# Four layers of linear attention and MLP on one core: turned blocks by way of DRAM, earlier queries, key maxima from PSUM, and row statistics on ScalarE

## The chip, the cores and the metric

One core of one Trainium2 chip runs the kernel. The metric is device time in microseconds (us). The engines go by the names of the profile: PE is TensorE, DVE VectorE, ACT ScalarE, POOL GpSimd, SP SyncE, which issues the DMA transfers. "PEld" is TensorE's weight load.

## The reference

2048 rows of 576 numbers pass through four layers, in turn a linear attention (A) and an MLP (B), with the same weights both times. Each layer adds its result to its input. Cut to what is computed:

```python
phi = lambda t: jnp.where(t > 0, t + 1, jnp.exp(t)) + 1e-6
def A(x, wqkv, wo):                 # 32 heads of 18
    q, k, v = split(x @ wqkv)
    pq, pk = phi(q), phi(k)
    kv  = einsum("bhsd,bhse->bhde", pk, v)
    z   = einsum("bhsd->bhd", pk)
    num = einsum("bhqd,bhde->bhqe", pq, kv)
    den = einsum("bhqd,bhd->bhq", pq, z) + 1e-6
    return (num / den) @ wo
def B(x, w1, b1, w2, b2):           # 576 -> 4608 -> 576
    return gelu(x @ w1 + b1) @ w2 + b2
x = x + A(layernorm(x)); x = x + B(layernorm(x))
x = x + A(layernorm(x)); x = x + B(layernorm(x))
```

The result is in bfloat16.

## The kernel before

Layers are counted 1 to 4 here; in the code `li` runs from 0 to 3, so layers 1 and 3 are attention (`layer_A`) and layers 2 and 4 MLP (`LayerB`). The 2048 rows are 16 tiles of 128 rows, or 4 blocks of 512. The weights stay in SBUF. `yT` holds the normalised rows of the current layer with the features on the partitions, as 5 groups of 128 (the fifth is half full; for the MLP its second half repeats the first). The rows themselves (float32) lie in DRAM as `x_d` between layers; `x_ring` has 5 buffers for rows that come back to be added, `xn` 3 buffers for new sums (`residual`, L372 to L386; the last layer's are called `xbf`).

**Attention.** The key loop goes over 16 tiles: keys (`k_proj`, L400, two halves of 288 columns), values (`v_proj`, L412 and L415), the product of keys and values of the tile before (L430), and from the fifth tile on one query product (`q_proj`, L436), in both layers. There are 20 query products, for 5 groups of heads by 4 blocks. Each half of the keys and each query product goes through phi (L350 to L354): ACT reads PSUM twice, for the exponential and for the number plus 1; DVE takes a minimum and the maximum of the two. Then come sums by head, the products `kvwo` (L481), and for each block the denominators (`den_stage`, L496, with the 1e-6 added by a product of one row at L500, reciprocals by DVE at L504) and five products `rden_ps` (`scale_stage`, L512) that spread the reciprocals over the rows of a group; ACT copies them and DVE multiplies the queries. The output loop has 16 tiles of ten products `wo_ps` (L523), with the reciprocal products of the next block, queries that are left, and the denominators of the block after next between them (at the third tile of a block).

**MLP.** Each of 4 blocks first makes 36 hidden groups (L624, written to `h_ps` and `hp_ps`, GELU by ACT at L620), then four output tiles of 72 products `m_ps` (L672). Two accumulators, `accA` and `accB`, take turns from tile to tile; so the third tile needs the first one's sum.

**Normalisation.** `LNPipe` takes a tile through steps, one at each `tick`: load, statistics on DVE (L272 to L283), the power -1/2 on POOL (L288), shift on POOL where needed (L292), normalisation (L303 on POOL or L307 on DVE) into one of three `y_ring` buffers, then the turn to `yT`. The first block of an MLP is fed from the output loop of the attention: normalised on POOL, turned by PE (`tp`, L324) and copied by ACT. All other blocks, and the attention's rows after the MLP, are turned by DVE in squares of 32 (L225) into one buffer, `turned`, and then moved by 16 transfers of 32 partitions (L232) inside SBUF. One `turned` buffer serves all of these, so a turn waits for the transfers of the block before.

The order of each engine's work is planned by the framework from the program order and the dependencies; PE's order is fixed as written. Some loads and statistics carry an extra order (`after`) behind the last residual sum: before, only those for the second block of an MLP. PSUM has three buffers "h" for keys, queries, denominators, reciprocals and hidden groups, one for `tp`, and the two accumulators.

Of the kernel before, what the change touches and what calls it, by code (L numbers as in the profile page):

```python
# [15 lines left out]
P = 128  # L16
# [18 lines left out]
def build(tc, A_x, A_wqkv, A_wo, B_w1, B_b1, B_w2, B_b2, out, dbg=None, n_layers=4):  # L35
    nc = tc.nc
    dbg = dbg or {}
    with ExitStack() as ctx:
        const = ctx.enter_context(tc.tile_pool(name="const", bufs=1))
        ps_h = ctx.enter_context(tc.tile_pool(name="ps_h", bufs=3, space=PSUM))  # L40
        ps_tp = ctx.enter_context(tc.tile_pool(name="ps_tp", bufs=1, space=PSUM))
# [21 lines left out]
        eps_row = const.tile([1, H], BF16, name="eps_row")  # L63
        one_row = const.tile([1, P], BF16, name="one_row")
# [9 lines left out]
        def inner_diag(tile_, lead, n):  # L74
# [10 lines left out]
            fill(eps_row, 1e-6),  # L85
# [25 lines left out]
        NV = 3  # L111
# [3 lines left out]
        turned = const.tile([P, 4 * KD, TPC, 32], BF16, name="turned")  # L115
        x_d = dpool.tile([NT, P, D], F32, name="x_d")

# [99 lines left out]
        state = dict(ycnt=0, vcnt=0, xl=0)  # L217
        pool_last = dict(norm=None)
        dve_last = dict(norm=None, sum=None, phi=None)

        def turn_rows(y, t, kind):

            c, j = divmod(t, TPC)
            nb = 4 * KD if kind == "B" else D // 32
            nc.vector.transpose(out=turned[:, 0:nb, j, :], in_=y[:, 0:32 * nb])  # L225
            if j < TPC - 1:
                return
            for i in range(4):
                for jj in range(4):
                    nk = KD if 16 + jj < nb else KD - 1  # L230
                    cols = slice(c * CB + i * P, c * CB + (i + 1) * P)
                    nc.sync.dma_start(  # L232
                        out=yT[32 * jj:32 * (jj + 1), 0:nk, cols],
                        in_=turned[32 * i:32 * (i + 1), jj:4 * (nk - 1) + jj + 1:4].rearrange("p k t c -> p k (t c)"))
# [8 lines left out]
        class LNPipe:  # L243
# [3 lines left out]
            def feed(self, xt, t, kind, norm_eng, evac_eng="dve", load_from=None, after=None):  # L247
                self.items.append(dict(stage=(0 if load_from is None else -1), xt=xt, t=t, kind=kind,
                                       norm=norm_eng, evac=evac_eng, load=load_from,
                                       after=after))  # L250

            def busy(self):
                return len(self.items)

            def tick(self, transposes=1):
                for it in list(self.items):
# [5 lines left out]
                    if st == -1:  # L262
# [5 lines left out]
                        it["xt"] = xn  # L268
                    elif st == 0:
# [20 lines left out]
                    elif st == 2 and it["norm"] != "dve":  # L290
                        nmr = work.tile([P, 1], F32, name="ln_nmr", bufs=4)
                        nc.gpsimd.tensor_scalar(out=nmr[:], in0=it["mv"][:, 0:1], scalar1=-1.0,  # L292
                                                scalar2=it["rstd"][:, 0:1], op0=ALU.mult, op1=ALU.mult)
                        it["nmr"] = nmr
                    elif st in (2, 3):
                        y = y_ring[state["ycnt"] % NY]
                        state["ycnt"] += 1
# [12 lines left out]
                        if it["kind"] == "B":  # L310
                            nc.gpsimd.tensor_copy(out=y[:, D:DPAD], in_=y[:, 4 * P:D])
# [3 lines left out]
                    elif st == 4:  # L315
                        y = it["y"]
                        t = it["t"]
                        if it["evac"] == "dma":
                            turn_rows(y, t, it["kind"])
                            self.items.remove(it)  # L320
                            continue
                        tp = ps_tp.tile([P, KD, P], BF16, name="tp", tag="tp")
                        for k in range(KD):
                            pe(nc.tensor.transpose(out=tp[:, k, :], in_=y[:, k * P:(k + 1) * P], identity=ident[:]))  # L324
                        if it["evac"] == "act":
                            nc.scalar.copy(out=yT[:, :, t * P:(t + 1) * P], in_=tp[:])
                        else:
                            nc.vector.tensor_copy(out=yT[:, :, t * P:(t + 1) * P], in_=tp[:])
                        self.items.remove(it)
                        continue  # L330
                    it["stage"] = st + 1

            def drain(self):
                while self.items:
                    self.tick()
# [4 lines left out]
        def warm_table(func, after):  # L340
            warm = nc.scalar.activation(out=act_dummy[:, 0:1], in_=neg_half[:, 0:1], func=func)
            tc.add_manual_dep(warm.ins, after, NOSYNC, reason="table of the next stage loaded early")

# [28 lines left out]
        def residual(li, t, halves):  # L372
            xo = xo_of.pop((li, t))
            last = (li == n_layers - 1)
            if last:
                xn = work.tile([P, 2 * D], BF16, name="xbf", tag="xn", bufs=3)[:, 0:D]
            else:
                xn = work.tile([P, D], F32, name="xn", tag="xn", bufs=3)[:]
            total = nc.vector.tensor_tensor(out=xn.rearrange("p (h n) -> p h n", h=2), in0=halves,  # L379
                                            in1=xo.rearrange("p (h n) -> p h n", h=2), op=ALU.add)  # L380
            dve_last["sum"] = total.ins.name
            if last:
                nc.sync.dma_start(out=out_f[t * P:(t + 1) * P, :], in_=xn)
                return None
            nc.sync.dma_start(out=x_d[t], in_=xn)
            return xn  # L386

        def layer_A(li, next_kind, pre_a1=None):
# [5 lines left out]
            def k_proj(t):  # L394
                tok = slice(t * P, (t + 1) * P)
                pk = blk.tile([P, D], BF16, name="pk", tag="blk")
                for half in range(2):
                    kp = ps_h.tile([P, 512], F32, name="k_ps", tag="h")
                    for k in range(KD):
                        pe(nc.tensor.matmul(kp[:, 0:HALF], lhsT=yT[:, k, tok],  # L400
                                         rhs=wqkv_sb[:, k, D + half * HALF: D + (half + 1) * HALF],
                                         start=(k == 0), stop=(k == KD - 1)))
                    phi_from_psum(kp[:, 0:HALF], pk[:, half * HALF:(half + 1) * HALF], P, HALF)
# [40 lines left out]
            for t in range(NT):  # L444
# [8 lines left out]
                if t >= 4:  # L453
                    q_proj(*q_left.pop(0))
# [62 lines left out]

            def wo_stage(t):
# [8 lines left out]
                if xn is not None and next_kind == "B" and t < TPC:  # L527
                    lnp.feed(xn, t, "B", "pool", "act")
# [20 lines left out]
            for t in range(NT):  # L549
# [9 lines left out]
                if j == 2 and c + 2 < NCA:  # L559
                    den_stage(c + 2)  # L560
                if t == NT - 3:
                    warm_table(ACT.Gelu_apprx_tanh, act_last["copy"])
# [12 lines left out]
        class LayerB:  # L575
# [70 lines left out]
            def run(self):  # L646
                li, next_kind = self.li, self.next_kind

                def feed_next(c, i):
                    if c + 1 < NCB:  # L650
                        t = (c + 1) * TPC + i
                        lnp.feed(None, t, "B", "dve", "dma", load_from=t, after=(dve_last["sum"] if c == 0 else None))

                for c in range(NCB):
# [12 lines left out]
                    for j in range(TPC):  # L667
                        t = c * TPC + j
                        acc = ps_acc.tile([P, 2, 512], F32, name="m2_ps", tag=next_acc())
                        for f in range(NF):  # L670
                            for half in range(2):
                                pe(nc.tensor.matmul(acc[:, half, 0:HALF], lhsT=hT[f][:, j * P:(j + 1) * P],  # L672
                                                    rhs=w2_sb[:, f, half * HALF:(half + 1) * HALF],
                                                    start=(f == 0), stop=(f == NF - 1)))
# [111 lines left out]
```

## Time and profile before

| what | us |
|---|---|
| median of 3 runs (lowest, highest) | 790.73 (789.31, 791.21) |
| the profiled execution, its time | 790.27 |
| the profiled execution, its span | 788.6 |
| PE busy in it | 769.9 |
| layer 1, to the MLP's first product | 0 to 112.10 |
| layer 2, four blocks | 112.10 to 393.84 |
| layer 3 | 393.84 to 491.91 |
| layer 4, first block | 491.91 to 573.47 |
| layer 4, last product of the last tile ends | 784.92 |

In timelines a line gives the start, the length, the engine, the source line, the operation with output and inputs, the count, and in brackets the idle time before it and what ended it. In groups it is the busy total, the mean length of one in ns, and the idle time before with its releasers. Instructions of one kind overlap somewhat, so work is counted here from start to start: 1.23 us for an output tile's ten products, 0.216 for a reciprocal product, 0.56 for a block's denominators, 0.28 for a tile's transposes, 1.08 for a query product. Line numbers in the profile before are those of the kernel before.

### The profile page before, as it was taken

How to read it: one execution, taken by the hardware profiler on the slowest of the kernel's cores; microseconds unless marked ns; L12 is line 12 of the kernel's file. 1: busy time of each engine (PE TensorE's matmuls, PEld its weight loads, DVE VectorE, ACT ScalarE, POOL GpSimd, SP SyncE). 2: the span in 40 equal slices, each digit the busy share in tenths (PEclk: the TensorE clock that was granted, in tenths of full speed). 3: DMA queues.
4: the chain of work that ended last, by engine and by line, in shares of the span. 5: the costliest groups of instructions: out<-in, count | busy, mean ns of one | idle time of the engine just before them, and what ended most of it. 6: DMA issues, size and time to landing. Idle time of an engine off the chain costs nothing.

```text
span 788.6 us, 15939 instructions
## 1 busy us (share of the span) xinstructions
PE 769.9 (98%) x6613; PEld 496.5 (63%) x6613; DVE 275.4 (35%) x710; ACT 341.7 (43%) x754; POOL 127.0 (16%) x211
## 2 busy tenths in 40 slices
PE   8999999999999999999999999996999999999998
PEld 5776654675477457547777756455744764675476
DVE  6786864044324413301355597544100000000000
ACT  5888636304610650362077774650056016304600
POOL 4671403013000301200000022311110010001000
PEclk9999999999999999999999999998899999999999
DMA  9990473122412331311120028443410110011000
GB/s 265 280 294 5 130 252 91 22 75 66 94 43 69 83 65 46 91 17 31 61 61 2 1 89 288 152 94 79 86 39 1 31 61 2 5 50 38 1 24 23
DMA packets 70642, 63.23 MB, mean 80 GB/s; under 512 B 37418, under 2 KB 55210, under 8 KB 70570
## 3 DMA queue, kind: packets, MB, share of 16 engines
q1 hardware_dynamic: 70570, 62.21, 28.1%
q8 instruction: 52, 0.85, 0.4%
q14 instruction: 20, 0.16, 0.1%
HBM read 39.38 MB, written 16.52 MB: 71 GB/s over the span
## 4 chain that ended last, share of the span: by engine, by line
PE 83%; DVE 7%; DMA 4%; SPq 3%; POOL 1%; issue 1%; ACT 1%; DVEq 0%; POOLq 0%
PE m_ps L672 34%; PE h_ps L624 17%; PE hp_ps L624 14%; PE q_ps L436 5%; PE k_ps L400 5%; PE v_ps L415 3%; SPq L232 3%; PE v_ps L412 2%; PE wo_ps L523 2%; DVE xn L379 1%; DMA x_d<-xn 1%; DVE turned L225 1%; PE kvacc L430 1%; DMA x_ring<-x_d 1%; DVE y_ring L307 1%
## 5 line engine op out<-in xcount | busy, mean ns | idle before, releaser
L672 PE MATMUL m_ps<-w_sb,hT 128*128 128x288 bf16 x2304 | 286.2, 287 | 8.5 <-DVE xbf L379 8.5
L672 PEld LDWEIGHTS <-hT 128*128 128x128 bf16 x2304 | 225.9, 98 | 69.8 <-issue 12.1
L624 PEld LDWEIGHTS <-w_sb 64*128 64x128 bf16 x2304 | 124.4, 94 | 136.6 <-issue 1.9
L624 PE MATMUL hp_ps<-yT,w_sb 64*128 64x512 bf16 x1152 | 178.0, 376 | 0.0
L629 ACT COPY relay_sb<-relay_sb 128x1 f32<-128x1 f32 x144 | 28.5, 198 | 276.6 <-PE h_ps L624 234.7
L624 PE MATMUL h_ps<-yT,w_sb 64*128 64x512 bf16 x1152 | 147.9, 376 | 0.0
L620 ACT ACTIVATE hT<-h_ps,b1T 128x512 bf16<-128x512 f32 x144 | 91.2, 684 | 44.5 <-PE h_ps L624 44.5
L288 POOL TENSOR_TENSOR ln_rstd<-ln_u,neg_half 128x1 f32<-128x1 f32 x64 | 36.2, 567 | 413.9 <-DVE ln_u L281 216.8
L620 ACT ACTIVATE hT<-hp_ps,b1T 128x512 bf16<-128x512 f32 x144 | 91.2, 693 | 0.0
L379 DVE TENSOR_TENSOR xbf<-m_ps,x_ring 128x576 bf16<-128x576 f32 x16 | 12.0, 754 | 221.2 <-PE m_ps L672 221.2
L369 POOL TENSOR_TENSOR x_ring<-x_ring,b_bc 128x576 f32<-128x576 f32 x32 | 41.1, 1291 | 203.7 <-DMA x_ring<-x_d 203.6
L379 DVE TENSOR_TENSOR xn<-m_ps,x_ring 128x576 f32<-128x576 f32 x16 | 12.1, 758 | 155.9 <-PE m_ps L672 155.9
L624 PE MATMUL h_ps<-yT,w_tail 64*128 64x512 bf16 x144 | 54.1, 376 | 0.0
L624 PE MATMUL hp_ps<-yT,w_tail 64*128 64x512 bf16 x144 | 54.1, 376 | 0.0
L436 PE MATMUL q_ps<-yT,wqkv_sb 128*126 128x512 bf16 (+1 forms) x200 | 50.0, 382 | 0.5 <-ACT phi_a L351 0.5
L225 DVE STREAM_TRANSPOSE turned<-y_ring 128x640 bf16<-128x640 bf16 (+1 forms) x40 | 32.2, 812 | 41.8 <-DMA yT<-turned 35.4
L523 PE MATMUL wo_ps<-kvwo,pq 126*128 126x288 bf16 (+1 forms) x320 | 43.7, 285 | 2.1 <-DVE xn L379 1.6
L400 PE MATMUL k_ps<-wqkv_sb,yT 128*128 128x288 bf16 x320 | 44.3, 286 | 0.0
L350 ACT ACTIVATE phi_e<-k_ps 128x288 bf16<-128x288 f32 x64 | 27.0, 421 | 34.8 <-PE k_ps L400 34.7
L352 DVE TENSOR_SCALAR phi_e<-phi_e 128x288 bf16<-128x288 bf16 (+2 forms) x104 | 30.7, 296 | 25.3 <-ACT phi_e L350 24.9
L523 PEld LDWEIGHTS <-pq 126*128 126x128 bf16 (+1 forms) x320 | 30.5, 97 | 13.7 <-issue 3.9
L400 PEld LDWEIGHTS <-yT 128*128 128x128 bf16 x320 | 30.9, 98 | 11.1
(90 smaller groups left out, 625.7 us busy)
## 6 DMA issues: line engine op xcount, KB each, us to landing
x_ring<-x_d SPq DMA_DIRECT2D x72, 288.0 KB, 3.1
x_d<-xn SPq DMA_DIRECT2D x48, 288.0 KB, 2.2
w_sb<-in_B_w_dram SPq DMA_DIRECT2D x6, 864.0 KB, 9.5
yT<-turned SPq DMA_DIRECT2D x128, 40.0 KB, 2.0
w_sb<-in_B_w_dram SPq DMA_DIRECT2D x9, 512.0 KB, 5.5
x<-in_A_x_dram SPq DMA_DIRECT2D x16, 144.0 KB, 4.1
x_ring<-in_A_x_dram SPq DMA_DIRECT2D x16, 144.0 KB, 3.4
out_dram<-xbf SPq DMA_DIRECT2D x16, 144.0 KB, 1.8
```

Source lines behind the costliest of these rows:

```text
L225: nc.vector.transpose(out=turned[:, 0:nb, j, :], in_=y[:, 0:32 * nb])
L288: nc.gpsimd.tensor_tensor(out=rstd[:], in0=it["u"][:], in1=neg_half[:], op=ALU.pow)
L352: nc.vector.tensor_scalar(out=e[0:rows, 0:n], in0=e[0:rows, 0:n], scalar1=1.0, scalar2=1e-6, op0=ALU.min, op1=ALU.add)
L369: nc.gpsimd.tensor_tensor(out=xo, in0=xo, in1=b2_bc[:], op=ALU.add)
L379: total = nc.vector.tensor_tensor(out=xn.rearrange("p (h n) -> p h n", h=2), in0=halves, in1=xo.rearrange("p (h n) -> p h n", h=2), op=ALU ...
L400: pe(nc.tensor.matmul(kp[:, 0:HALF], lhsT=yT[:, k, tok], rhs=wqkv_sb[:, k, D + half * HALF: D + (half + 1) * HALF], start=(k == 0), stop=( ...
L436: pe(nc.tensor.matmul(qp[0:GR[g], :], lhsT=wqkv_sb[:, k, GO[g]:GO[g] + GR[g]], rhs=yT[:, k, c * CA:(c + 1) * CA], start=(k == 0), stop=(k ...
L523: pe(nc.tensor.matmul(wp[:, half, 0:HALF], lhsT=pq[(g, c)][0:GR[g], j * P:(j + 1) * P], rhs=kvwo[g][0:GR[g], half * HALF:(half + 1) * HALF ...
L620: act_last["gelu"] = nc.scalar.activation(out=to, in_=ps, func=ACT.Gelu_apprx_tanh, bias=b1T[:, f:f + 1], scale=1.0).ins.name
L624: mm = pe(nc.tensor.matmul(dst[n], lhsT=wt, rhs=mv, start=(seen[n] == 0), stop=(seen[n] == 8)))
L629: relay = nc.scalar.copy(out=relay_sb[:, 1:2], in_=relay_sb[:, 0:1])
L672: pe(nc.tensor.matmul(acc[:, half, 0:HALF], lhsT=hT[f][:, j * P:(j + 1) * P], rhs=w2_sb[:, f, half * HALF:(half + 1) * HALF], start=(f == ...
```

## The change

- The turned rows of a block (18 squares instead of 20) go to DRAM in 4 transfers, into one of two buffers `y_d`; three ticks later one transfer brings back the first 512 features and one or two the last 64. The copy on POOL that repeated the last 64 features is left out for these blocks.
- Turns come behind the last residual sum in the order, and so do loads and statistics of every block of the MLP, not only of the second.
- "h" gets four PSUM buffers; `tp` has none of its own and takes one of these. `xn` gets four buffers, `v_ring` two instead of three.
- In layer 3 queries start at the third tile (index 2), and the denominators come at the second tile of a block instead of the third. In layer 1 both stay.
- In layer 3 the second half of each tile's keys goes through `phi_by_dve`: one exponential by ACT, then DVE adds 1 and takes the maximum straight from PSUM.
- The first block of an MLP gets its statistics from ACT: one pass with Identity that adds up the row, a mean on POOL, one pass with Square that adds up the squares, a step on POOL. The feeding is one tile later, and there is one more tick at these tiles.
- The product that adds 1e-6 has 126 rows, all but the first zero, instead of one.
- The very last tile's 72 products run half by half, and each half is summed and stored by itself.

The diff, cut to its core:

```diff
-        ps_h = ctx.enter_context(tc.tile_pool(name="ps_h", bufs=3, space=PSUM))
-        ps_tp = ctx.enter_context(tc.tile_pool(name="ps_tp", bufs=1, space=PSUM))
+        ps_h = ctx.enter_context(tc.tile_pool(name="ps_h", bufs=4, space=PSUM))
...
-        eps_row = const.tile([1, H], BF16, name="eps_row")
-        one_row = const.tile([1, P], BF16, name="one_row")
+        eps_row = const.tile([126, H], BF16, name="eps_row")
+        one_row = const.tile([126, P], BF16, name="one_row")
...
-        NV = 3
+        NV = 2
...
-            nc.vector.transpose(out=turned[:, 0:nb, j, :], in_=y[:, 0:32 * nb])
+            turn = nc.vector.transpose(out=turned[:, :, j, :], in_=y[:, 0:D])
+            if dve_last["sum"] is not None:
+                tc.add_manual_dep(turn.ins, dve_last["sum"], NOSYNC, reason="rows are turned behind the sums")
...
+            home = y_d[state["turns"] % 2]
+            state["turns"] += 1
             for i in range(4):
-                for jj in range(4):
-                    nk = KD if 16 + jj < nb else KD - 1
-                    cols = slice(c * CB + i * P, c * CB + (i + 1) * P)
-                    nc.sync.dma_start(
-                        out=yT[32 * jj:32 * (jj + 1), 0:nk, cols],
-                        in_=turned[32 * i:32 * (i + 1), jj:4 * (nk - 1) + jj + 1:4].rearrange("p k t c -> p k (t c)"))
+                nc.sync.dma_start(out=home[:, :, i * P:(i + 1) * P].rearrange("j r n -> r j n"),
+                                  in_=turned[32 * i:32 * (i + 1), :, :, :].rearrange("r j t c -> r j (t c)"))
+            landing.append([3, home, c, kind])
+
+        def land(now=False):
+            for it in list(landing):
+                it[0] -= 1
+                if it[0] > 0 and not now:
+                    continue
+                _, home, c, kind = it
+                landing.remove(it)
+                cols = slice(c * CB, (c + 1) * CB)
+                nc.sync.dma_start(out=yT[:, 0:KD - 1, cols],
+                                  in_=home[0:16, :, :].rearrange("(k jj) r n -> (jj r) k n", jj=4))
+                for hi in range(2 if kind == "B" else 1):
+                    nc.sync.dma_start(out=yT[64 * hi:64 * (hi + 1), KD - 1, cols],
+                                      in_=home[16:18, :, :].rearrange("jj r n -> (jj r) n"))
...
+                    elif st == 0 and it["stats"] == "act":
+                        mv = it["mv"] = work.tile([P, 2], F32, name="ln_mv", bufs=6)
+                        y = it["y"] = self.slot()
+                        nc.scalar.activation(out=y[:, 0:D], in_=it["xt"][:, 0:D], func=ACT.Identity,
+                                             accum_out=mv[:, 0:1])
+                        nc.gpsimd.tensor_scalar(out=mv[:, 0:1], in0=mv[:, 0:1], scalar1=-1.0 / D, scalar2=None,
+                                                op0=ALU.mult)
+                        it["stage"] = 0.5
+                        continue
+                    elif st == 0.5:
+                        u = it["u"] = work.tile([P, 1], F32, name="ln_u", bufs=4)
+                        mv = it["mv"]
+                        nc.scalar.activation(out=it["y"][:, 0:D], in_=it["xt"][:, 0:D], func=ACT.Square,
+                                             bias=mv[:, 0:1], accum_out=mv[:, 1:2])
+                        nc.gpsimd.tensor_scalar(out=u[:], in0=mv[:, 1:2], scalar1=(1.0 + EPS) / D, scalar2=EPS * EPS,
+                                                op0=ALU.mult, op1=ALU.add)
...
-                        tp = ps_tp.tile([P, KD, P], BF16, name="tp", tag="tp")
+                        tp = ps_h.tile([P, 512], F32, name="tp", tag="h")
...
+        def phi_by_dve(ps_ap, out_ap, rows, n):
+            e = work.tile([P, 512], BF16, name="phi_e", bufs=3)
+            act_last["exp"] = nc.scalar.activation(out=e[0:rows, 0:n], in_=ps_ap, func=ACT.Exp).ins.name
+            nc.vector.tensor_scalar(out=e[0:rows, 0:n], in0=e[0:rows, 0:n], scalar1=1.0, scalar2=1e-6,
+                                    op0=ALU.min, op1=ALU.add)
+            top = nc.vector.scalar_tensor_tensor(out=out_ap, in0=ps_ap, scalar=C1, in1=e[0:rows, 0:n],
+                                                 op0=ALU.add, op1=ALU.max)
...
+            parts = [slice(h * HALF, (h + 1) * HALF) for h in range(2)] if last and t == NT - 1 else [slice(0, D)]
...
+                    phi = phi_by_dve if li > 0 and half == 1 else phi_from_psum
...
-                if t >= 4:
+                if t >= (4 if li == 0 else 2):
                     q_proj(*q_left.pop(0))
...
-                if j == 2 and c + 2 < NCA:
+                if j == (1 if li > 0 else 2) and c + 2 < NCA:
                     den_stage(c + 2)
+                if next_kind == "B" and 1 <= t <= TPC:
+                    lnp.feed(sums[t - 1], t - 1, "B", "pool", "act", stats="act")
+                    lnp.tick(transposes=0)
...
-                        lnp.feed(None, t, "B", "dve", "dma", load_from=t, after=(dve_last["sum"] if c == 0 else None))
+                        lnp.feed(None, t, "B", "dve", "dma", load_from=t, after=dve_last["sum"])
...
+                        by_half = li == n_layers - 1 and t == NT - 1
+                        steps = [(f, half) for half in range(2) for f in range(NF)] if by_half else \
+                            [(f, half) for f in range(NF) for half in range(2)]
```

## The prediction

> **What bounds the kernel now.** The page comes first: TensorE (PE) is busy nearly the whole span, so only PE's idle time and PE's slow time can be won. The view of waits, PE alone, names the idle time (microseconds in total, times, longest):
>
> ```profile
> PE 769.9 (98%) x6613; PEld 496.5 (63%) x6613; DVE 275.4 (35%) x710; ACT 341.7 (43%) x754; POOL 127.0 (16%) x211
> ...
> PE m_ps L672 <- DVE xbf L379: 8.5, 1, 8.5
> PE wo_ps L523 <- DVE xn L379: 1.6, 3, 1.1
> PE rden_ps L512 <- DVE rden L504: 0.7, 2, 0.3
> PE q_ps L436 <- ACT phi_a L351: 0.5, 2, 0.2
> ```
>
> One wait of 8.5 us is most of it: PE's second MLP product waits for a residual sum of VectorE (DVE). PE's timeline places it in the last layer's first block, and the table by stretches (PE, PEld, DVE, ACT, POOL busy; granted clock; DMA share; GB/s) shows what follows it:
>
> ```profile
> 526.98 17.81 PE L672 MATMUL m_ps<-w_sb,hT 128*128 128x288 bf16 x144
> 553.34 20.19 PE L672 MATMUL m_ps<-w_sb,hT 128*128 128x288 bf16 x144 [8.54 <-DVE xbf L379]
> ...
> 544.80:553.30 8.50, 0.00 (x0) 0.00 (x0) 6.80 (x16) 0.00 (x0) 1.53 (x4) 0.69 0.22 69
> 553.30:557.00 3.70, 3.66 (x16) 2.32 (x16) 0.65 (x1) 0.00 (x0) 0.00 (x0) 0.50 0.35 55
> 557.00:560.00 3.00, 3.00 (x21) 2.17 (x20) 0.00 (x0) 0.00 (x0) 0.00 (x0) 0.79 0.41 65
> 560.00:573.50 13.50, 13.50 (x113) 10.61 (x112) 0.76 (x1) 0.00 (x0) 2.55 (x2) 1.00 0.40 97
> ```
>
> After the wait the granted clock is 0.50, then 0.79, then 1.00: 288 products that took 35.39 us in every other block took 573.53 - 526.98 = 46.55. The wait costs 11.16 us, not 8.54. DVE's timeline says why it is late:
>
> ```profile
> 525.32 1.57 DVE L225 STREAM_TRANSPOSE turned<-y_ring 128x640 bf16<-128x640 bf16 x2 [7.83 <-DMA yT<-turned]
> ...
> 545.42 1.57 DVE L225 STREAM_TRANSPOSE turned<-y_ring 128x640 bf16<-128x640 bf16 x2 [7.70 <-DMA yT<-turned]
> ...
> 552.57 1.38 DVE L379 TENSOR_TENSOR xbf<-m_ps,x_ring 128x576 bf16<-128x576 f32 x2
> ```
>
> The first sum was ready at 535.8 (half of the 17.81) and ran at 552.57. DVE's queue had the normalisations of blocks 2, 3 and 4 ahead of it, each held for the 16 small transfers of the block before (11 us of issuing on SP, 0.60 us each). The seven other MLP blocks take 70.46 us with no wait: they hold nothing to win. The two attention layers lose more, in small pieces. In layer 3, from the end of the first output tile (463.54) to the MLP (491.91), 28.37 us pass for 26.09 of PE work: 15 output tiles of 1.23, 15 reciprocal products of 0.216, two denominators of 0.56, four transposes of 0.28, two queries of 1.08. Layer 1 needs 29.45 (82.65 to 112.10).
>
> **Part by part, against the profiled execution (span 788.6, time 790.27; the median of the three runs shown is 790.73).**
>
> *Loads and turns behind the sums.* In the changed order DVE has only one block's four turns ahead of the last layer's first sum. In the trace these end at 512.7, so the sum runs at 535.8 and the wait goes with its slow clock: **-11.16**. What could be late next is the new trip through DRAM. Four writes at 0.60 each, or at 3.6 times that if each of their 576 pieces costs what one of 160 did, are 2.4 to 8.7 us of issuing, then 2.0 to land (yT<-turned), three reads of at most 2.2 each to issue and 3.1 to land (x_ring<-x_d). From 512.7 that ends by 533; the block is read at 562.4. In layer 2 the cover is of the same size, and in layer 3 the last tile's rows (sum at 394.8) land by about 420 for key tile 13 at 437. Cost 0 while the trip is under some 45 us; beyond it, every us counts in each block. On SP the read waits for its writes with row stores queued behind; the next store is due over 10 us later, so 0.
>
> *Queries from tile 3 (layer 3).* Two queries, 2.2 us, move from the output loop to the key loop. PE work is unchanged, but in the output loop they were cover. ScalarE (ACT) is busy 40.70 of the 55 us of the key loop, so the two earlier tiles don't wait. *Key maxima from PSUM* take 0.3 us per tile from ACT and put at most 0.75 - 0.34 on DVE (sum of 576 against the 288 maximum); both have room, and PE does not wait in that loop: 0, within 0.2.
>
> *Four PSUM buffers.* The third reciprocal product and a query wait for a buffer before the first output tile: 1.14 us for 0.43 of work at 456.97 and 0.91 for 0.49 at 460.08, some 1.1 us per layer. With a fourth buffer both go, then the first output tile waits for its scaled queries (ready 0.6 earlier at best). I take 0.5 per layer: **-1.0** (0 to -2.2).
>
> *Statistics by ACT.* This is the adverse part. POOL, by groups, and ACT's copy of the same width:
>
> ```profile
> L288 POOL TENSOR_TENSOR ln_rstd<-ln_u,neg_half 128x1 f32<-128x1 f32 x64 | 36.2, 567 | 413.9 <-DVE ln_u L281 216.8 <-DVE ln_u L283 196.8 <-DVE ln_mv L278 0.3
> L292 POOL TENSOR_SCALAR ln_nmr<-ln_mv,ln_rstd 128x1 f32<-128x1 f32 x22 | 10.9, 497 | 2.4
> L311 POOL COPY y_ring<-y_ring 128x64 bf16<-128x64 bf16 x32 | 8.7, 273 | 13.7 <-DVE y_ring L307 10.5 <-DVE ln_u L283 2.7
> L303 POOL TENSOR_SCALAR y_ring<-xn,ln_rstd,ln_nmr 128x576 bf16<-128x576 f32 x8 | 7.1, 888 | 0.8
> ...
> L488 ACT CAST kvwo<-kvwo_ps 126x576 bf16<-126x576 f32 x4 | 2.6, 644 | 0.0
> ```
>
> Per tile: Identity 0.65 (L488), Square 0.75 (0.1 more for the bias, as L620's 0.69 against L514's 0.59), two new POOL steps of 0.27 (L311, the nearest; 0.57 at most, L288). Counted from the end of the first output tile, layer 3: sum 1.05, two copies and Identity on ACT 2.15, mean 2.5, two more copies and Square 3.95, then POOL with 0.1 between steps 7.3. PE reaches the tile's transpose at 5.33 (three output tiles, five reciprocal products, a denominator): it waits 2.0. Each further tile needs mean, Square, u, power, shift and normalisation in turn, for POOL takes the next mean behind this normalisation: 3.75 us. Tile 2 is ready at 11.05 for PE at 9.3: 1.75. Tile 3 is ready in time, but Square of tile 4 waits for POOL with reciprocal copies behind it on ACT, and the transpose waits for the buffer of one: 1.1. Tile 4: 0. So 23.93 of work and 4.85 of waits: 28.8 against 28.4, and with the 2.2 moved ahead layer 3 gets **+2.65**. The same count for layer 1, where two queries cover: waits 0, 1.5, 0.8, 0, so 28.45 against 29.45; its wait of 1.1 for a store of rows should go with the fourth row buffer, perhaps not wholly: **-0.7**. With 0.57 for the POOL steps each layer gains 1.5 more.
>
> The Trainium skill speaks against this part ("ScalarE: Activation LUTs", Rules for kernel authors): adding and multiplying belong on VectorE. Its prices (What ACT_TABLE_LOAD costs: 186 ns and 0.833 ns an element, 93 ns more for a pointer) make the passes 0.67 and 0.76, an estimate, and the sum 0.1 to 0.2 longer.
>
> *Last tile by halves.* After the last product (784.92) come a sum of 0.76 and a store. A half sum is 0.45 (between 0.23 for 72 columns and 0.75 for 576): **-0.35** (0 to -0.6). The other edits (buffers, masks, eps rows) stand beside PE work of 4 us a tile: 0.
>
> **Sum:** -11.16 - 1.0 + 2.65 - 0.7 - 0.35 = -10.56; 790.27 - 10.56 = **779.7**.
>
> **Rivals.** (a) *The chain of statistics is quicker.* Power, shift and normalisation alone are 2.25 us a tile, ACT's passes 1.4; at a period of 3.2 layer 3 comes out 2.8 shorter and layer 1 1.4: 775.5. (b) *POOL's steps are as dear as its power:* 3 us more, 782.7; with no gain from the buffers and in layer 1, 784.4. (c) *Something still stands before the first sum,* say a turn held for the DRAM writes: the wait stays, and with the rest the time is 779.7 + 11.2 = 790.9. Against it: in DVE's changed order the next turn comes behind all four sums of the block. (d) *Slower.* The period of the statistics is so long that PE's wait at a transpose drops the clock too. Six periods stand on the path; at 5.4 us they add 9.9 and tile 2's waits pass 3.1 in both layers. The trace has 1.00 through a wait of 1.12 and 0.50 after 8.54, so a drop between is open; at 2.6 each (11.16 - 8.54) the time is 779.7 + 9.9 + 5.2 = 794.8, and it decides from a period of about 4.7 on if they drop. Only accumulating passes of twice the copy's 0.65 would do that.
>
> The Trainium skill ("TensorE: Matmul & The Clock Gate", Why this matters for your kernels) puts the limit of idle time at some 3 us; the trace agrees with 1.12 and 8.54 on its two sides. By that rule waits of 2.0 cost themselves alone and the sum stays 779.7; with a drop at each of the three waits over 1.4 us it would be 787.5.
>
> **How the numbers follow.** Forecast 0.58; (a) 0.15; (b) 0.14; (c) 0.06; (d) 0.07. (a) and (b) set the range, 775.0 to 785.0, which leaves out (c) and (d). About 0.3% (2.4 us) is what a measurement of this kernel can tell from no change: faster 0.87, same 0.06, slower 0.07.
>
> **What would show it.** Right: the wait for xbf is gone, the clock is 1.00 after 527, all eight MLP blocks take 70.46; transposes wait for POOL's rows, 1 to 2 us twice in layer 3; the output loop of layer 3 takes 28 to 30 us. Wrong: a wait over 3 us at a transpose, sums late behind turns, or a block's first product waiting for yT.

## The result, and the profile after

The changed kernel takes **783.83 us** (median of 4 runs, 783.38 to 785.12) against 790.02 us of the kernel before on the same chip (4 runs, 789.22 to 791.21): a ratio of 0.9923, interval 0.9904 to 0.9942, so 6.2 us (0.8%) faster. The forecast was 779.7, with a range of 775.0 to 785.0. The profiled execution of after is the 785.12 one, with a span of 783.4.

TensorE's (PE's) waits, largest first (total, times, longest):

```profile
PE tp L363 <- POOL y_ring L341: 6.2, 5, 2.7
PE tp L363 <- ACT rden_bc L568: 1.9, 2, 1.3
...
PE wo_ps L579 <- DVE kvwo L540: 0.9, 2, 0.5
```

The wait of 8.5 us for xbf has gone. In its place transposes wait for POOL's rows, five times, 6.2 us in all, and the longest of these, 2.7 us, is not in an output loop: it is at the very start.

Layer 4's first block, in after's chain that ended last (the work that set the end of the span, followed back; start, length) and in VectorE's (DVE's) timeline:

```profile
533.03 35.39 PE m_ps L733 x288
603.48 35.39 PE m_ps L733 x288
```

```profile
516.73 0.78 DVE L227 STREAM_TRANSPOSE turned<-y_ring 128x576 bf16<-128x576 bf16 x1
541.99 0.76 DVE L431 TENSOR_TENSOR xbf<-m_ps,x_ring 128x576 bf16<-128x576 f32 x1 [24.48 <-PE m_ps L733]
```

The block's 288 products take 35.39 us, as in every other block, where before they took 46.55. DVE now stands idle for 24.48 us until PE has a sum for it; before, PE stood still for DVE.

Every run below is laid out by the same marks, so the table says where time went. Times are of the profiled executions, from one stage's start to the next: *start* ends at the second half of layer 1's last value product; *value to output* runs from there to the first output tile, layers 1 and 3 together; an *output loop* goes from its first output tile's start to the MLP (1.4 us more than the prediction's count from that tile's end); *layer 4* from its first MLP product to the end of the span. Layer 2 takes 281.73 or 281.74 in every run and is left out.

| run | start | value to output | output loop 1 | key loop 3 | output loop 3 | layer 4 | span | median us | ratio to before |
|---|---|---|---|---|---|---|---|---|---|
| before | 67.21 | 28.05 | 30.87 | 54.25 | 29.79 | 296.69 | 788.6 | 790.02 | |
| after | 70.73 | 27.24 | 31.18 | 56.46 | 30.54 | 285.51 | 783.4 | 783.83 | 0.9923 [0.9904, 0.9942] |
| e1 | 68.02 | 28.05 | 30.79 | 54.26 | 29.83 | 285.52 | 778.2 | 779.45 | 0.9862 [0.9846, 0.9879] |
| e2 | 70.48 | 27.24 | 31.22 | 56.46 | 30.57 | 285.49 | 783.2 | 783.77 | 0.9919 [0.9904, 0.9934] |
| e3 | 70.66 | 27.24 | 28.85 | 56.45 | 27.46 | 285.50 | 777.9 | 778.00 | 0.9850 [0.9831, 0.9868] |
| e4 | 67.12 | 27.25 | 31.22 | 56.45 | 30.56 | 285.46 | 779.8 | 781.52 | 0.9890 [0.9874, 0.9906] |
| e5 | 66.87 | 27.24 | 28.84 | 56.45 | 27.44 | 285.52 | 774.1 | 776.12 | 0.9814 [0.9800, 0.9827] |
| e6 | 67.27 | 27.25 | 28.85 | 56.46 | 27.43 | 285.01 | 774.0 | 775.75 | 0.9810 [0.9797, 0.9824] |
| e7 | 69.40 | 27.26 | 29.86 | 56.46 | 27.47 | 285.52 | 777.7 | 779.01 | 0.9850 [0.9837, 0.9864] |
| e8 | 69.26 | 27.24 | 31.20 | 54.26 | 31.04 | 285.47 | 780.2 | 782.02 | 0.9888 [0.9874, 0.9901] |
| e9 | 71.71 | 28.05 | 30.37 | 54.25 | 30.02 | 295.87 | 792.0 | 794.02 | 1.0038 [1.0024, 1.0052] |
| e10 | 66.74 | 27.24 | 28.84 | 54.25 | 28.67 | 284.92 | 772.4 | 774.40 | 0.9793 [0.9780, 0.9805] |
| e11 | 67.04 | 27.84 | 28.85 | 56.45 | 27.44 | 284.94 | 774.3 | 776.27 | 0.9815 [0.9802, 0.9828] |
| e12 | 67.50 | 27.25 | 30.42 | 56.46 | 29.54 | 285.00 | 777.9 | 779.40 | 0.9853 [0.9841, 0.9866] |

Of the ledger before to after, layer 4 won 11.2 and the stretches before the output tiles 0.8; the start lost 3.5, layer 3 lost 3.0 (2.2 of it in the key loop) and layer 1 lost 0.3. (The medians of before beside the four groups of runs, after, e1 to e4, e5 to e8 and e9 to e12, were 790.0, 789.9, 790.7 and 790.9.)

### The profile page after: what moved, and what is told of

Read it like the earlier page. It is cut to its first block, busy times and chain, and to the rows that moved or that the text cites. A ratio compares the mean times of both kernels' runs of the same rounds, so it can differ in the third digit from the quotient of the medians.

```text
span 783.4 us, 15790 instructions
## 1 busy us (share of the span) xinstructions
PE 767.0 (98%) x6613; PEld 495.6 (63%) x6613; DVE 270.6 (35%) x679; ACT 345.8 (44%) x770; POOL 122.3 (16%) x201
## 4 chain that ended last, share of the span: by engine, by line
PE 91%; ACT 2%; DVE 2%; POOL 2%; DMA 1%; issue 1%; SPq 0%; DVEq 0%; POOLq 0%; ACTq 0%
PE m_ps L733 36%; PE h_ps L683 20%; PE hp_ps L683 16%; PE k_ps L453 5%; PE q_ps L490 4%; PE wo_ps L579 3%; PE v_ps L469 3%; PE v_ps L466 2%; PE kvacc L484 1%; ACT rden_bc L568 1%; DMA x_ring<-x_d 1%; PE tp L363 1%; DMA x<-in_A_x_dram 1%; POOL y_ring L341 1%; PE rden_ps L566 1%
## 5 line engine op out<-in xcount | busy, mean ns | idle before, releaser
L431 DVE TENSOR_TENSOR xbf<-m_ps,x_ring 128x576 bf16<-128x576 f32 (+1 forms) x17 | 12.2, 722 | 218.2 <-PE m_ps L733 218.2
L683 PEld LDWEIGHTS <-w_tail 64*128 64x128 bf16 x288 | 27.1, 94 | 17.1
L398 ACT ACTIVATE phi_e<-k_ps 128x288 bf16<-128x288 f32 x48 | 20.2, 420 | 34.5 <-PE k_ps L453 34.3
L400 DVE TENSOR_SCALAR phi_e<-phi_e 128x288 bf16<-128x288 bf16 (+2 forms) x88 | 26.5, 302 | 25.2 <-ACT phi_e L398 25.1
```

The source lines that it names most:

```text
L400: nc.vector.tensor_scalar(out=e[0:rows, 0:n], in0=e[0:rows, 0:n], scalar1=1.0, scalar2=1e-6, op0=ALU.min, op1=ALU.add)
L431: total = nc.vector.tensor_tensor(out=xn[:, cols].rearrange("p (h n) -> p h n", h=nh), in0=ps, in1=xo[:, cols].rearrange("p (h n) -> p h n ...
L683: mm = pe(nc.tensor.matmul(dst[n], lhsT=wt, rhs=mv, start=(seen[n] == 0), stop=(seen[n] == 8)))
```

## The experiments

### Which part removes the wait of 8.5 us: e1 and e2

The edges are the extra orders that put loads, statistics and turns behind the last residual sum. e1 is the kernel before with the edge on loads and statistics alone; e2 is the changed kernel without any of the added edges, the trip through DRAM left in.

```
e1:  -  lnp.feed(None, t, ..., after=(dve_last["sum"] if c == 0 else None))
     +  lnp.feed(None, t, ..., after=dve_last["sum"])
e2:  the reverse of e1's line, and in turn_rows
     -  tc.add_manual_dep(turn.ins, dve_last["sum"], NOSYNC, ...)
```

> The kernel before with one edit: in every block, not only in the first, the loads of the next block's rows and their statistics stand behind the last residual sum (no trip through DRAM, no other part of the change). Theory A, VectorE's queue order is the whole gain: layer 4 block 1 falls from 81.6 to 70.4 us, the wait for xbf and the slow clock behind it go, nothing else moves, so 790.0 - 11.1 = 778.9 us, which is 4.9 faster than the whole change. Rival B, the sixteen small transfers are then in the way at a later place (they hold the turns 7.8 us each time): a first product of a block waits for yT, and the time stays within 1 us of 783.8 or above.

> The changed kernel with both kinds of edges taken out: turns are not held behind sums, and loads only in block 1, as before; the trip through DRAM stays. Theory A, only the edges help: three blocks of turns stand ahead of layer 4's first sum again, the wait of 8.5 us and the slow clock return, 783.8 + 11.1 = 794.9 us. Rival C, the trip alone is enough: it holds VectorE for 2.4 us of issuing and some 3 of landing where the sixteen transfers held it for 11, so a block of turns takes some 12 us in place of 20, the last turn ends at about 512.7 + 24 = 537 in the time of the trace before, ahead of the 544.8 at which TensorE began to wait, and the time stays at 783.8.

Measured: e1 779.45, as theory A had it, and layer 4 falls to 285.52; DVE waits 23.75 us for its first sum there, which runs at 536.78, 9.03 us after the block's first product, as in after. e2 783.77, as rival C had it: layer 4 stays at 285.49. **Either part alone removes the wait; together they remove it once.** e1's one line is faster than the whole change by 4.4 us. How e2 does it, in DVE's timeline of layer 4 (block 2's last turn, the first two of block 3, the first two and the last of block 4, then the first sum):

```profile
516.81 0.78 DVE L227 STREAM_TRANSPOSE turned<-y_ring 128x576 bf16<-128x576 bf16 x1
...
522.81 1.44 DVE L227 STREAM_TRANSPOSE turned<-y_ring 128x576 bf16<-128x576 bf16 x2 [0.44 <-DMA y_d<-turned]
...
535.59 1.44 DVE L227 STREAM_TRANSPOSE turned<-y_ring 128x576 bf16<-128x576 bf16 x2
...
542.07 0.78 DVE L227 STREAM_TRANSPOSE turned<-y_ring 128x576 bf16<-128x576 bf16 x1
542.77 0.72 DVE L429 TENSOR_TENSOR xbf<-m_ps,x_ring 128x576 bf16<-128x576 f32 x1
```

Three blocks' turns still stand ahead of the sum, in the same wrong order as before. But a turn now waits 0.44 us for the four writes that read its buffer, where it waited 7.83 for the sixteen, so a block of turns takes 12.8 us (522.81 to 535.59) instead of 20.1. The sum runs at 542.77, 0.95 us later than in after, counted from the block's first product, and PE needs its buffer only some 7 us later (in before it began to wait 17.8 us after that product, here 550.6): it never waits.

### What the start lost: e4 and e9

Nothing in the change was meant for the first 20 us. In after, ScalarE's (ACT's), DVE's and PE's timelines there read:

```profile
9.39 0.41 ACT L398 ACTIVATE phi_e<-k_ps 128x288 bf16<-128x288 f32 x1
11.22 0.58 ACT L471 CAST v_ring<-v_ps 128x504 bf16<-128x504 f32 x1 [1.43 <-PE v_ps L469]
...
12.61 0.42 ACT L399 ACTIVATE phi_a<-k_ps 128x288 bf16<-128x288 f32 x1
```

```profile
13.06 0.31 DVE L402 TENSOR_TENSOR pk<-phi_a,phi_e 128x288 bf16<-128x288 bf16 x1 [2.56 <-ACT phi_a L399]
...
13.93 0.45 DVE L310 BATCH_NORM_STATS2 ln_st<-x 128x6 f32<-128x288 bf16 x1
```

```profile
17.57 0.56 PE L363 MATMUL tp<-ident,y_ring 128*128 128x128 bf16 x5 [2.72 <-POOL y_ring L341]
17.92 1.26 PE L466 MATMUL v_ps<-wqkv_sb,yT 128*128 128x252 bf16 x5
```

ACT idles 1.43 us for a value product, copies it, and only then computes the phi_a of key tile 2 that DVE waits for. DVE's statistics of the fourth tile stand behind that, POOL's normalisation behind them, and PE's transpose behind POOL. Before, phi_a came ahead of the copies, the statistics began at 11.97 and the transpose waited 0.42:

```profile
10.66 0.41 ACT L351 ACTIVATE phi_a<-k_ps 128x288 bf16<-128x288 f32 x1 [0.64 <-DVE pk L354]
...
11.55 0.60 ACT L417 CAST v_ring<-v_ps 128x504 bf16<-128x504 f32 x1
```

```profile
11.97 0.45 DVE L272 BATCH_NORM_STATS2 ln_st<-x 128x6 f32<-128x288 bf16 x1
```

```profile
15.61 0.45 PE L324 MATMUL tp<-ident,y_ring 128*128 128x128 bf16 x5 [0.42 <-POOL y_ring L303]
```

The three value slots had become two, and the order came out differently; that the scheduler's modelled times moved with the fewer fills on POOL is argued from the code, the order and its price are what the next two runs show.

```
e4 (on after):   -  for vr in v_ring:
                 +  for vr in v_ring + v_ring[:1]:      # one slot is filled twice
e9 (on before):  -  NV = 3
                 +  NV = 2
```

> The changed kernel with one value slot filled twice at the start, so that POOL has three slots to fill as in the kernel before and ScalarE's instructions of the first tiles stand in the order of before (second maximum of a key tile ahead of the value copies); two buffers stay. Theory O, ScalarE's order made the start longer: the fourth tile's transpose waits 0.4 us in place of 2.7, the clock does not drop, the start falls from 70.2 to 66.7 us against the profiled run of after and by some 2 us against its median, 781.8. Rival L, the start is late because the third rows' load landed later or because two slots are too few: 783.8 within 0.5.

> The kernel before with one edit: two value slots in place of three. Theory O, with one slot less to fill POOL's modelled time at the start is shorter, ScalarE's order of the first tiles becomes that of the changed kernel, and the start grows from 67.2 to 69.3 to 70.7 us without any other part of the change: 790.2 + 2.3 = 792.5. Rival: the start is late only together with another part (the shared buffers of the transposes): 790.2 within 0.5.

Measured: e4 781.52, start 67.12; e9 794.02 (3.1 slower than its 790.94 of before), start 71.71. e4's order of PE and SP is that of after; only ACT's order of these few instructions, DVE's next to them and the three extra fills on POOL differ. So theory O holds from both sides, and two slots are enough once the order is right. In e4:

```profile
10.61 0.41 ACT L399 ACTIVATE phi_a<-k_ps 128x288 bf16<-128x288 f32 x1 [0.60 <-DVE pk L402]
...
11.60 0.57 ACT L471 CAST v_ring<-v_ps 128x504 bf16<-128x504 f32 x1
```

```profile
15.61 0.45 PE L363 MATMUL tp<-ident,y_ring 128*128 128x128 bf16 x5 [0.40 <-POOL y_ring L341]
```

Of e9's longer start, 0.95 us lie ahead of the first transpose (6.80 against 5.85), where DVE waited 0.89 us for the second tile's rows. Only this execution has a trace, so whether the others of e9 (791.56 to 795.67) paid that too is not shown, and 3.1 is a looser price than e4's 2.3.

### What the statistics on ScalarE cost: e3, e7 and e5

```
e3 (on after):  -  sums[t] = xn   ...   lnp.feed(sums[t - 1], t - 1, "B", "pool", "act", stats="act")
                +  lnp.feed(xn, t, "B", "pool", "act")          # in wo_stage, as before
e7 (on after):  -  nc.gpsimd.tensor_scalar(out=mv[:, 0:1], ...)   nc.gpsimd.tensor_scalar(out=u[:], ...)
                +  nc.vector.tensor_scalar(out=mv[:, 0:1], ...)   nc.vector.tensor_scalar(out=u[:], ...)
e5:             e3 and e4 together
```

> The changed kernel with the statistics of the first MLP block on VectorE again, fed right after the sum as before. Theory S, the chain of ScalarE passes and POOL steps sets the transposes' waits: its period of 3.4 us falls to the 2.3 us of POOL's three steps, the output loop of layer 3 goes from 29.1 to some 27.0 us and that of layer 1 from 29.8 to 28.5, so 783.8 - 3.3 = 780.5 us. Rival P, the waits are POOL's own steps behind VectorE's scaled queries whoever takes the statistics: both loops stay within 0.4 us, 783.8.

> The changed kernel, statistics' passes still on ScalarE, but the two small steps between them (negative mean, variance) on VectorE in place of POOL. Theory (POOL's queue): POOL takes a tile's mean only behind the normalisation of the tile before, so its steps set the period of 3.4 us; without them the period falls to some 2.6 and the two loops lose about half of the 5.4 us that e3 won: 781.0. Rival (passes): ScalarE's two passes with their read-outs, between reciprocal copies, set it; 783.8 within 0.7. Rival (VectorE's queue): the small steps wait there behind sums and scaled queries of 0.6 to 1.4 us, and it gets slower, 785.

> The changed kernel with both e3 and e4: first MLP rows' statistics by VectorE, and the start in the order of before. Theory S+O, the two losses lie in different stages and add: e3 gave 5.8 and e4 2.3 of 783.8, so 775.7 us, with a start of 67.1, output loops of 27.3 and 25.9. Rival: VectorE's order at the start moves again with the statistics' code, one of the two gains is lost, 778.0.

e3 also feeds each row one tile earlier and leaves out the extra tick; e7 keeps both as in after.

Measured: e3 778.00, more than theory S had: loop 1 falls by 2.3 and loop 3 by 3.1. e7 779.01, more than its POOL theory had: with the passes still on ACT but the two small steps off POOL, loop 3 is as short as with DVE's statistics (27.47) and loop 1 gets 1.3 of its 2.3 back (29.86). e5 776.12, against 775.7 for the sum of both gains: they add within 0.4. POOL's timeline in after's output loop 3 shows the chain:

```profile
474.52 0.82 POOL L341 TENSOR_SCALAR y_ring<-xn,ln_rstd,ln_nmr 128x576 bf16<-128x576 f32 x1
475.43 0.23 POOL L294 TENSOR_SCALAR ln_mv<-ln_mv 128x1 f32<-128x1 f32 x1
...
476.64 0.19 POOL L303 TENSOR_SCALAR ln_u<-ln_mv 128x1 f32<-128x1 f32 x1 [0.81 <-ACT y_ring L301]
476.92 0.58 POOL L326 TENSOR_TENSOR ln_rstd<-ln_u,neg_half 128x1 f32<-128x1 f32 x1
477.60 0.27 POOL L331 TENSOR_SCALAR ln_nmr<-ln_mv,ln_rstd 128x1 f32<-128x1 f32 x1
477.97 0.82 POOL L341 TENSOR_SCALAR y_ring<-xn,ln_rstd,ln_nmr 128x576 bf16<-128x576 f32 x1
```

and ACT's, the other end of the same loop:

```profile
472.58 0.68 ACT L292 ACTIVATE y_ring<-xn 128x576 bf16<-128x576 f32 x1
473.15 0.20 ACT L292 ACTIVATION_READ_ACCUMULATOR y_ring<-xn 128x1 f32 x1
...
475.69 0.78 ACT L301 ACTIVATE y_ring<-xn,ln_mv 128x576 bf16<-128x576 f32 x1 [1.87 <-POOL ln_mv L294]
```

Tile 2's sum of elements is read out at 473.35, but POOL takes its mean (0.23 us) only at 475.43, behind tile 1's normalisation; Square waits 1.87 us for it, and POOL then idles 0.81 for Square. Neither engine is busy, each waits for the other in turn: a row every 3.45 to 4.24 us. In e7 POOL's normalisations begin at 472.02, 474.32, 476.83 and 480.19: a row every 2.30, 2.51 and 3.36 us, and no Square waits for a mean there:

```profile
474.05 0.78 ACT L301 ACTIVATE y_ring<-xn,ln_mv 128x576 bf16<-128x576 f32 x1
```

So in layer 3 it is not the passes (0.68 and 0.78 us) that cost, for e7 keeps them. Nor is it the length of POOL's two small steps alone: 0.23 and 0.19 us a row, where the mean period fell from 3.79 to 2.72. What cost is that they stand in POOL's queue. In layer 1 this explains 1.3 of the 2.3; whether the other 1.0 is due to the passes or to the later feeding is not shown.

### The queries, the buffers and the last tile: e8, e10, e11, e12, e6

```
e8 (on after), e10 (on e6):  -  if t >= (4 if li == 0 else 2):   +  if t >= 4:
e11 (on e6):  ps_h bufs 4 -> 3, and a PSUM pool of one buffer for the transposes alone
e12 (on e6):  tag="xn", bufs 4 -> 3
e6 (on e5):   the last tile's second half in a PSUM tile of its own, read by the second half sum
```

> The changed kernel with layer 3's queries from key tile 5 again, so that two of them (2.2 us of TensorE work) are left for its output loop. Theory (cover): the loop has 3.4 us of waits at its transposes that the two queries can fill, the key loop falls from 56.5 to 54.3 and the output loop grows by at most 0.5: 783.8 - 1.8 = 782.0. Rival (no cover): the waits stand at other tiles than the queries, the loop grows by 2.2, 783.8.

e8: 782.02, as the cover theory had it: the key loop gives 2.2 back and the output loop takes 0.5.

> As e6 (statistics by VectorE, start in the old order, two accumulators at the end), with layer 3's queries from key tile 5. Theory (cover): with statistics by VectorE the output loop of layer 3 still has 1.9 us over its TensorE work, 1.5 of it one wait for a residual sum, and a late query can fill it: 775.9 - 1.5 = 774.4. Rival (wash): the loop of the kernel before was 28.2 with late queries and is 25.9 now with 2.2 less work in it, so the waits stand elsewhere: the key loop falls by 2.2, the output loop grows by 2.2, 775.9.

e10: 774.40, again the cover: 2.2 back, 1.24 taken. That it met the expected 774.4 is partly luck: these two stages win 0.97 and not 1.5, and another 0.53 of the profile lies in the start (66.74 against 67.27), where nothing was edited. **This is the fastest version**, 16.5 us under its before (790.94), 1.3% under the changed kernel by the two ratios.

> As e6, with three shared PSUM buffers and one for the transposes alone, as before. Theory B (my term of four buffers): only the stretch from the last value product to the first output tile changes, from 13.6 to 14.0 us in each attention layer, 775.9 + 0.8 = 776.7. Rival: in the output loops the shared ring makes transposes wait for buffers of reciprocals (1.9 us in the changed kernel), and with a buffer of their own these loops win as much as the stretch loses: 775.9 within 0.4.

e11: 776.27, theory B with a smaller size: each stretch grows by 0.30 rather than 0.4, and the output loops do not move. Against e6 (another group of runs) the intervals overlap; the reading rests on the table's stretches. Of the 0.81 that both stretches lost from before to after, the fourth buffer thus explains 0.6; which other edit gave the rest was not tested.

> As e6, with three row buffers for the residual sums in place of four. Theory R (my term of 1.1 in layer 1): a sum of layer 1's output loop waits for the store of rows again, the loop grows from 27.3 to 28.3 us and the one of layer 3 by less, 775.9 + 1.0 = 776.9. Rival: the wait of before was VectorE's queue and not the store, 775.9 within 0.3.

e12: 779.40, and larger than the theory: loop 1 grows by 1.57 and loop 3 by 2.11. In DVE's timeline of layer 1 the sums are held by both users of a row:

```profile
95.76 0.76 DVE L431 TENSOR_TENSOR xn<-wo_ps,x_ring 128x576 f32<-128x576 f32 x1 [1.02 <-POOL y_ring L341]
...
106.94 0.76 DVE L431 TENSOR_TENSOR xn<-wo_ps,x_ring 128x576 f32<-128x576 f32 x1 [1.27 <-DMA x_d<-xn]
```

In this version, with the statistics on DVE, the fourth buffer frees the sums from POOL's normalisation as well as from the store.

> As e5, and the last tile's two halves in two PSUM tiles of their own. In after both half sums begin together, behind the last product: theory T says that is because they read one PSUM tile whose last writer is the second half's product; with two tiles the first half's sum and store run under the second half's products, and from the end of the last product to the end of the span 0.35 us less pass (some 3.3 in place of 3.7). Rival: the end is the store's own landing, about 2 us, which the first store does not shorten, and the second half's sum alone is as late as before: under 0.1. The median alone can't tell 0.35 us; the profile's tail can.

e6: layer 4 ends 0.51 us sooner in the profile, 285.01 against 285.52; the medians can't tell it. The last sums, in after and in e6 (SPq is SP's queue of transfers):

```profile
779.88 0.82 DVE L431 TENSOR_TENSOR xbf<-m_ps,x_ring 128x288 bf16<-128x288 f32 x2 [8.06 <-PE m_ps L733]
```

```profile
766.57 0.46 DVE L431 TENSOR_TENSOR xbf<-m_ps,x_ring 128x288 bf16<-128x288 f32 x1 [3.65 <-PE m_ps L733]
767.05 4.69 SPq L435 DMA_DIRECT2D out_dram<-xbf  x2
770.92 0.46 DVE L431 TENSOR_TENSOR xbf<-m_ps,x_ring 128x288 bf16<-128x288 f32 x1 [3.90 <-PE m_ps L733]
```

In after both halves run back to back behind the last product; with two PSUM tiles the first is done 4 us earlier. Theory T holds.

## Why the prediction was right in direction and 4.1 us short

By its own terms, from the profiled executions:

| term of the sum | predicted | measured |
|---|---|---|
| loads and turns behind the sums (layer 4) | -11.16 | -11.18 |
| four PSUM buffers (both stretches before the output tiles) | -1.0 | -0.81 |
| layer 3: key loop / output loop | +2.2 / +0.45 | +2.21 / +0.75 |
| layer 1's output loop | -0.7 | +0.31 |
| last tile by halves | -0.35 | 0 |
| other edits | 0 | +3.52 (start) |
| sum | -10.56 | -5.20 |

Output loop 3's +0.45 is +0.41 by the prediction's own rows (23.93 + 4.85 - 28.37); nothing hangs on it.

*Right.* The wait of 8.5 and the slow clock behind it were one price of 11.2. What the prediction did not see is that the change holds two cures: it ascribed the gain to the order and gave the shorter hold of the trip no effect; e2 shows that the trip alone would have done. Rival (c) did not come: block 2's last turn ended 24.5 us before the sum was ready, and no later turn stood ahead of it.

*The step that failed* is "The other edits (buffers, masks, eps rows) stand beside PE work of 4 us a tile: 0." The number of value slots is among them. That they stand beside PE work is true from about 20 us on; at the start PE has nothing ahead of the fourth tile's transpose, and the edit's price was not the buffer's but a new order on ACT. Undoing only that (e4) gives 2.3 us by the medians; doing only that (e9) costs 3.1. It is over half of the 4.1 us by which the forecast missed; the terms below make up the rest: layer 1 by 1.0, the last tile by 0.35, layer 3 by 0.3 and the buffers by 0.2. Of the 3.52 in the table about 1.4, by estimate, is a slow clock that only the profiled one of after's four executions shows (see the last section). No rival named the start. The stated range was set by two rivals, and neither came; that it still holds 783.83 is owed to its width, and that much is luck.

*Mis-sized:* layer 1. The row buffers were put at 1.1 and are worth 1.57 there, and 2.11 in layer 3, where the prediction gave them nothing (e12, on a version with DVE's statistics). The statistics on ACT take 2.3 and 3.1 back (e3). The prediction's net of the two was too good by 1.0 in layer 1 and by 0.3 in layer 3. Its waits in layer 3 (2.0, 1.75, 1.1, 0) came out as 1.13, 1.06, 1.26 and 0; the two transposes held for POOL took 0.72 in place of 0.44 on top:

```profile
475.40 0.72 PE L363 MATMUL tp<-ident,y_ring 128*128 128x128 bf16 x5 [1.13 <-POOL y_ring L341]
...
478.85 0.72 PE L363 MATMUL tp<-ident,y_ring 128*128 128x128 bf16 x5 [1.06 <-POOL y_ring L341]
...
484.51 0.44 PE L363 MATMUL tp<-ident,y_ring 128*128 128x128 bf16 x5 [1.26 <-ACT rden_bc L568]
```

The mechanism it named, "POOL takes the next mean behind this normalisation", is what e7 shows; its period of 3.75 came out as 3.45 to 4.24. In layer 1 the named waits at transposes are 0.99 and 0.60 and do not make up the loss; the rest is spread over gaps too small to be named, and stays open.

*Missed:* the last tile. The sum of the first half needed a PSUM tile of its own (e6: 0.51, against 0.35 predicted). *Rivals:* (a) and (b) did not come. (d), the slow clock at a wait in an output loop, did not come there (no wait over 1.3), but its mechanism did at the start, in the profiled execution. The rows of 126 for the 1e-6 and the earlier denominators were not run alone; the key loop of layer 3 with half its keys through `phi_by_dve` is as long in e8 (54.26) as before (54.25), so that part cost nothing there.

The Trainium skill ("ScalarE: Activation LUTs", Rules for kernel authors) would have left these statistics on VectorE, and e3 agrees, with 5.8 us. The price per pass is not why: the estimates from its prices in the prediction, 0.67 and 0.76, stand beside means of 0.68 and 0.78 in the trace of after.

## What to carry to other kernels

Price an edit at the places where no work covers it: two value slots in place of three cost nothing in the steady key loop of layer 3 (54.25 in e9 and before), and 2 to 3 us at a start where the scheduler's order hung on them, so compare each engine's order there, too. A step of 0.2 us between passes of another engine can cost as much as the queue ahead of it, not only its own length; give such a step to an engine whose queue is short. When a change brings two cures for one wait, run each alone: here one line of it was worth more than the whole.

## What the runs showed of the hardware

*Whether a wait of about 2.5 us slowed the clock went by where it fell in a rhythm of 3.41 us.* The fourth tile's transpose waited 2.54 us by the trace in e2, e7, e8 and e9, 2.67 in e3 and 2.72 in after. Windows of 2.4 us behind it (PE, PEld, DVE, ACT, POOL busy; granted clock; DMA share; GB/s), first e2, then e7:

```profile
17.60:20.00 2.40, 2.40 (x19) 1.74 (x16) 0.00 (x0) 0.93 (x2) 2.06 (x5) 0.61 0.87 257
```

```profile
17.60:20.00 2.40, 2.11 (x23) 1.81 (x24) 0.31 (x2) 1.08 (x2) 2.19 (x5) 1.00 0.99 307
```

In e2 the clock falls, in e7 it does not. The records of the granted clock in the traces, with the times of its changes, show a difference. In e2 it goes to 1.00 at 4.46, stands at 0.50 from 18.11 to 21.52, and is 1.00 again after that. In after, e3 and e9 it stands at 0.50 from 17.78, 18.48 and 18.45, each time for 3.41 us. In all four the drop comes 13.65 us, four times 3.41, after the rise, and in layer 4 of before the slow clock lasted 10.24, three times 3.41. So in these traces the clock changed only on a grid of 3.41 us, which lies elsewhere in each execution. In the four executions that dropped, the stretch of the grid before the drop holds 2.42 to 2.72 us in which PE idles. In e7 and e8 the clock rose at 6.92 and 6.65, so a line of the grid (17.16 and 16.89) cuts the wait in two, and the stretch before it holds only 1.81 and 1.67. In none of the 14 traces did the clock fall from 1.00, while the program ran, after a stretch with 1.91 us of idle time or less. That fits all six executions; no run shifted the grid by itself.

A drop cost 1.1 to 1.5 us at the start, on top of the wait: starts of 70.48 to 70.73 with it (e2, e3, after), 69.26 and 69.40 without (e8, e7). Three of after's four runs show a mean granted clock of 1.000 and the profiled one 0.997, so by the starts of e8 and e7 its median run paid about 2.1 for the start and not 3.5, an estimate. The Trainium skill ("TensorE: Matmul & The Clock Gate", What's actually happening) says that the activity window is 3413 ns long, runs freely and does not start with the kernel, which agrees with these records; it lets the clock fall after at least one idle window, and here 2.42 us idle out of 3.41 were enough.

*A pass of ACT with an accumulated result is two instructions:* in after's 16 passes an ACTIVATE of 0.67 to 0.79 us and a read-out (ACTIVATION_READ_ACCUMULATOR) of 0.18 to 0.23. *POOL's steps on one column* took 0.23 and 0.28 us in the mean in after with constants alone (8 each; one took 0.79), 0.43 with a scalar from memory (22 of them) and 0.56 for a power (64).
